# Casts and copies on Pool behind gates, in a planned kernel of attention and two Strassen stages

## The chip, the cores and the metric

The kernel runs on one core of a Trainium2 chip. The metric is the device time of one execution in microseconds (us): the median of the kernel before, over three runs, is 797.23 (795.54 to 802.38).

## What is computed

Sliding-window attention with a linear bias, then two feed-forward blocks over its output. Shapes: q, k, v are (4, 8, 576, 64); w1, w2 (512, 1024), w3 (1024, 1024), w_out (1024, 512); the last two weights (512, 2048) and (2048, 512). All is fp32.

```python
scores = scale * np.matmul(q, k.transpose(0, 1, 3, 2))
bias = slopes[:, None, None] * (-np.abs(rel).astype(np.float32))[None, :, :]
mask = (rel >= 0) & (rel < window)                       # window = 128
scores = np.where(mask, scores + bias[None], -1000000000.0)
scores = scores - np.max(scores, axis=-1, keepdims=True)
attn = np.exp(scores)
attn = attn / (np.sum(attn, axis=-1, keepdims=True) + 1e-09)
x = np.matmul(attn, v)                                   # then reshaped to (2304, 512)
x = (((x @ w1) * (x @ w2)) @ w3) @ w_out
h = np.maximum(x @ w_in, 0.0)
out = h * h @ w_out2
```

## The kernel before

Heads are worked in 16 pairs of one batch (`add_pair`). For a pair, TensorE forms the windowed scores in PSUM (`p_qk`, L473), VectorE adds the bias and takes the row minimum of the negated scores in one custom instruction out of PSUM (`l_min`, L443: "minima" below, ten for a pair), ScalarE takes the exponential with a row sum (`l_exp`, L451), VectorE adds 1e-9 to the sums (the guard, L458) and takes the reciprocal (L459), both in `l_sum`, and VectorE or ScalarE scales the rows (`l_norm`, L267 or L269: "normalizations"). TensorE transposes the result (`p_tr`, L509), ScalarE copies it out of PSUM (`l_pt`), and TensorE multiplies by v (`p_pv`, L533, and `p_pvl`, L549). Some blocks of v are needed on the other half of the partitions, and `l_v` (L417, L418) copies them there. The results leave PSUM in `t_xh`. Pairs before the seventh (`SM`) have guard and reciprocal for each head, later ones once for both.

Beside the attention part the kernel prepares w3 x w_out, since the first block's last two matmuls have no nonlinearity between them. The weights arrive as 64-bit words; `add_words` turns one load of 1 MB (eight of w3, four of w_out, in `load_order`) into fp32 with a Prelu on ScalarE (`conv_g`, L343), a shift on VectorE or ScalarE (`conv_s`, L352) and a merge on VectorE (`conv_m`, L358), and then splits it into two fp32r halves: the cast (`split_h`) and the residue, a subtraction on VectorE (`split_l`, at L211). TensorE multiplies the halves in triples (`p_w34`, L203 to L205): 64 triples in all, of low rank, that fill its idle time. Dummy matmuls fill longer idle times up to 90 us (`p_fill`, L581).

When all pairs are done, the PSUM pools of the attention part are closed (`open_pp`) and products of Strassen's form begin (`add_seven`, L993 to L995, then `p_r` and `p_o`): seven products for each block, of weights and activations that VectorE combines (L778) and ScalarE and VectorE split.

The order on every engine is made at build time by `Plan.run`. Each task has a rank, the engines that it may run on with a cost each, its dependences and the buffers that it takes and gives. The planner takes the ready task of the lowest rank among those that could start soonest; `bias` is added to the cost of an engine in this choice. A cost key "D" means VectorE from SBUF, "d" VectorE from PSUM or small operands, "p" Pool; "D" and "p" exclude each other through `lock`. The engines run their lists in order; semaphores are set by the framework.

```python
bias = dict(d=1.75, D=0.15, a=0.30, p=6)
...
add("sh" + k, rank + 0.1, w_split(1024), lambda e: split_h(key, e), ["cn" + k], ["sp" + k], ["raw" + k])
add("sl" + k, rank + 0.1, w_tt(1024), lambda e: split_l(key, e), ["sh" + k], [], ["raw" + k])
...
add(f"cv{m}", r + RANK["vv"], {"p": 1.1, "D": 0.5}, lambda e: l_v(m, e), [f"ldv{m}"])
```

Of the kernel before, what the change touches and what calls it, by code (L numbers as in the profile page):

```python
# [15 lines left out]
RANK = dict(w34=9, vv=14, w0=-18, c0=-20, cj=6, h0=-42, hs=7, su=6, w12=60, wa=23, wl=5, wb=0, x0=26, mg=5, mgs=1.70, wo=1132, gg=6, yq=1166)  # L16
# [11 lines left out]
SM = 7  # L28
# [4 lines left out]
class Plan:  # L33
# [11 lines left out]
    SLACK = dict(ldw=1, lx=2, ldi=3.0, ldo=3.0, mb=2.00, lg=2.00, lw=4.00, ldv=1.0)  # L45
    STORES = ("sx", "sw", "sg", "sy", "ms", "ss")

    bias = dict(d=1.75, D=0.15, a=0.30, p=6)

    def __init__(self, caps, lat):  # L50
        self.caps, self.lat = caps, lat
        self.tasks = {}
        self.holds = {}

# [6 lines left out]
    def add(self, name, rank, where, fn, deps=(), takes=(), gives=(), keep=0):  # L61

        assert name not in self.tasks, name
        self.tasks[name] = (rank, where, fn, tuple(deps), tuple(takes), tuple(gives), keep)

    def run(self):
# [16 lines left out]
        now = 0  # L83
        while ready:
            cands = []
            for n in ready:
# [13 lines left out]
                for q, w in where.items():  # L100
                    e = q.lower()
# [7 lines left out]
                    for d in deps:  # L109
                        t = max(t, end[d] + self.late(d) * (e != "dma") + (0.0 if on[d] == e and (e != "dma" or d[:2] not in self.STORES) else self.lat[on[d]]))  # L110
# [28 lines left out]
            ready.remove(n)  # L139
            for h in takes:  # L140
                p = pool[self.holds[h][0]]
                p.remove(min(p))
            fin = t + w
            end[n], on[n] = fin, e
            free[e] = fin
            if q in "Dp":
                lock = fin
            for h in gives:
                left[h] -= 1
                last[h] = max(last[h], fin + (self.lat[e] + 0.5 if e == "dma" else 0.0))  # L150
                if left[h] == 0:
                    pool[self.holds[h][0]].append(last[h] + 0.1)
            order.append((n, e, t, fin))
            for u in users.get(n, ()):
                need[u] -= 1
                if need[u] == 0:
                    ready.add(u)
# [5 lines left out]
def fused_kernel(  # L163
# [65 lines left out]
    zero = at.tile([128, 128], F32, name="zero")  # L229
# [54 lines left out]
    def w_split(n):  # L284
        return {"a": 0.12 + n * 0.00088, "p": 0.25 + n * 0.0009}
# [7 lines left out]
    def w_tt(n, engs="Dp"):  # L293
# [3 lines left out]
    def w_ts(n, engs="Dap"):  # L297
# [1285 lines left out]
```

## Time and profile before

| what | value |
|---|---|
| median of three runs | 797.23 us |
| the profiled execution | 796.22 us |
| its span, first to last instruction | 794.4 us |
| granted TensorE clock, of full speed | 0.999 |
| TensorE busy / VectorE / ScalarE / Pool | 783.1 / 632.6 / 513.7 / 3.9 us |

Busy times of TensorE overlap: its matmuls are pipelined and their ends are modelled, so a full share doesn't mean that it had no time to spare. Times in the rows are us from the span's start, unless marked ns. The durations of VectorE and ScalarE reach into the next instruction's, too: what an instruction takes of the engine is read from one start to the next.

### The profile page before, as it was taken

The page shows a single profiled execution, that of the slowest core. Times are in us where ns is not written, and L with a number is a line of the kernel's source. Part 1 is how long each engine was busy: PE and PEld are TensorE (multiplying, and loading weights), DVE is VectorE, ACT ScalarE, POOL GpSimd, SP SyncE. Part 2 cuts the span into 40 slices and gives each one's busy share as a digit, 9 for nine tenths or more (in the row PEclk, how much of TensorE's full clock was granted, in tenths as well). Part 3 has the DMA queues.
Part 4 walks back from the last instruction along what each step waited for, and adds up shares of the span by engine and source line. Part 5 has one row for each costly group of instructions (what it writes and reads, how often), then busy time and mean ns, then how long its engine had stood idle before and what let it go on. Part 6 is the DMA issues. An engine that isn't in the chain of part 4 may idle for free. (4 is left out here: it accounts for less than half of the span.)

```text
span 794.4 us, 17410 instructions
## 1 busy us (share of the span) xinstructions
PE 783.1 (99%) x6664; PEld 741.7 (93%) x6664; DVE 632.6 (80%) x1366; ACT 513.7 (65%) x1102; POOL 3.9 (0%) x19
## 2 busy tenths in 40 slices
PE   8999998999999999999999999999999999999998
PEld 6677776899999999999999999999999999999998
DVE  6999999999887878998889975424678997777762
ACT  7999999775444444655565766546777786666631
POOL 1000000000000000000000000000000000000000
PEclk9999999999999999999999999999999999999999
DMA  9994757635687879666664552535654766454201
GB/s 254 269 310 134 238 161 198 210 122 176 229 269 253 306 241 315 229 222 200 211 207 134 202 189 100 189 120 173 212 193 143 216 176 171 135 140 135 86 27 34
DMA packets 108850, 149.50 MB, mean 188 GB/s; under 512 B 9440, under 2 KB 87776, under 8 KB 106720
## 3 DMA queue, kind: packets, MB, share of 16 engines
q1 hardware_dynamic: 108768, 148.40, 59.1%
q8 instruction: 52, 0.85, 0.4%
q14 instruction: 30, 0.25, 0.1%
HBM read 97.78 MB, written 50.59 MB: 187 GB/s over the span
## 5 line engine op out<-in xcount | busy, mean ns | idle before, releaser
L208 ACT ACTIVATE d<-xa 128x288 f32<-128x288 f32 x128 | 51.6, 409 | 108.9 <-PE xa L995 100.6
L1253 DVE TENSOR_TENSOR D<-xb,D 128x384 f32<-128x384 f32 (+1 forms) x62 | 32.2, 520 | 53.2 <-ACT D L208 26.4
L208 ACT ACTIVATE D<-xa 128x384 f32<-128x384 f32 (+1 forms) x93 | 42.3, 457 | 36.1 <-PE xa L1191 32.4
L451 ACT ACTIVATE e<-e,st 128x192 f32<-128x192 f32 (+1 forms) x144 | 62.3, 439 | 4.9 <-DVE st L443 4.7
L211 DVE TENSOR_TENSOR ww<-fq,ww 128x1024 fp32r<-128x1024 f32 x35 | 42.6, 1223 | 26.3 <-ACT ww L208 26.1
L208 ACT ACTIVATE ww<-fq 128x1024 fp32r<-128x1024 f32 x35 | 37.1, 1059 | 35.7 <-PE xa L1191 19.5
L993 PE MATMUL xa<-xB,u 128*128 128x288 f32 x192 | 57.0, 297 | 0.5 <-DVE d L1042 0.4
L995 PE MATMUL xa<-xB,u 128*128 128x288 f32 x192 | 56.8, 296 | 0.0
L994 PE MATMUL xa<-xB,u 128*128 128x288 f32 x192 | 56.1, 292 | 0.0
L778 DVE TENSOR_TENSOR xA<-xA 128x256 f32<-128x256 f32 (+2 forms) x89 | 52.1, 611 | 0.7
L1326 ACT ACTIVATE D<-D 128x384 f32<-128x384 f32 x72 | 37.3, 521 | 23.0 <-DVE D L1253 22.8
L1014 DVE TENSOR_TENSOR d<-xb,d 128x288 f32<-128x288 f32 x80 | 36.2, 453 | 13.1 <-PE xb L995 8.1
L443 DVE CUSTOM_DVE_ANT_0 e<-s,bw 128x192 f32<-128x192 f32 (+1 forms) x128 | 40.5, 351 | 0.6 <-PE s L473 0.3
L473 PE MATMUL s<-qk 64*64 64x128 f32 (+2 forms) x768 | 36.6, 282 | 2.9 <-DMA qk<-in_qk_dram 2.2
L473 PEld LDWEIGHTS s<-qk 64*64 64x64 f32 x768 | 26.8, 133 | 12.1 <-issue 5.4
L993 PEld LDWEIGHTS xa<-xB,u 128*128 128x128 f32 x192 | 36.1, 188 | 1.0 <-DVE d L1042 0.6
L509 PE MATMUL t<-ident,e 128*128 128x128 f32 x208 | 35.6, 283 | 1.3 <-ACT pt L208 1.1
L509 PEld LDWEIGHTS t<-ident,e 128*128 128x128 f32 x208 | 24.3, 141 | 13.3 <-ACT pt L208 5.9
L994 PEld LDWEIGHTS xa<-xB,u 128*128 128x128 f32 x192 | 36.5, 190 | 0.0
L995 PEld LDWEIGHTS xa<-xB,u 128*128 128x128 f32 x192 | 36.0, 188 | 0.0
L1189 PE MATMUL xa<-yA,v 128*128 128x384 f32 x104 | 35.3, 340 | 0.0
L1191 PE MATMUL xa<-yA,v 128*128 128x384 f32 x104 | 35.2, 339 | 0.0
(267 smaller groups left out, 2920.0 us busy)
## 6 DMA issues: line engine op xcount, KB each, us to landing
s_scr<-D SPq DMA_DIRECT2D x95, 192.0 KB, 1.9
u<-in_w2io_dram SPq DMA_DIRECT2D x32, 512.0 KB, 6.0
xA<-s_scr SPq DMA_DIRECT2D x20, 512.0 KB, 5.4
qk<-in_qk_dram SPq DMA_DIRECT2D x32, 288.0 KB, 5.0
g_scr<-d SPq DMA_DIRECT2D x64, 144.0 KB, 3.1
xA<-g_scr SPq DMA_DIRECT2D x16, 576.0 KB, 5.2
raw<-in_w3t_dram SPq DMA_DIRECT2D x8, 1024.0 KB, 7.2
raw<-in_w_dram SPq DMA_DIRECT2D x8, 1024.0 KB, 7.2
```

The costliest lines, as they stand in the source:

```text
L208: nc.scalar.activation(out=o, in_=i, func=ACTF.Copy)
L211: eng.tensor_tensor(out=o, in0=a, in1=b, op=ALU.subtract)
L443: nc.vector.tensor_tensor_reduce(out=part_of(m, x, rows), in0=ps, in1=bias, op0=ALU.add, op1=ALU.min, scale=-0.125, scalar=3.0e38, accum_o ...
L451: nc.scalar.activation(out=e, in_=e, func=ACTF.Exp, bias=st[:, 0, x:x + 1], scale=-1.0, accum_out=st[:, 1, x:x + 1],)
L473: nc.tensor.matmul(HD[2 * m + r]["s"][g][o, c:c + w], t[h, 0, 64 * q:64 * q + 64], t[h, 1, 64 * k:64 * k + w], start=True, stop=True,)
L509: nc.tensor.transpose(o, e[:, u:u + 2, :].rearrange("p u c -> p (u c)"), ident)
L778: ENG[e].tensor_tensor(out=o(oi), in0=a(ai), in1=b(bi), op=op)
L993: nc.tensor.matmul(o, wh, xh, start=start and c == 0, stop=False, skip_group_check=True)
L994: nc.tensor.matmul(o, wh, xl, start=False, stop=False, skip_group_check=True)
L995: nc.tensor.matmul(o, wl, xh, start=False, stop=c == len(todo) - 1, skip_group_check=True)
L1014: nc.vector.tensor_tensor(out=sb[K, o], in0=sb[K, a], in1=sb[K, o], op=op)
L1326: nc.scalar.activation(out=x, in_=x, func=ACTF.Relu)
```

## The change

The split's cast of w3 and w_out (all loads but the first) and the two copies of v, which become two tasks, may now run on Pool, and there only behind a gate: when the planner places a minimum on VectorE, it looks how long the series of minima from it on will be (`series`), and puts such tasks on Pool as fit into that series by their costs; each gets a dependence on the VectorE instruction ahead of the series (`prevd`), which becomes a semaphore wait of Pool. `after` holds these tasks back until a given pair's minima have been placed. Guard and reciprocal become two tasks (`l_sum`, `l_inv`), and an instruction on VectorE that needs its predecessor's result is charged `OWN` = 0.117 us more, so that the planner puts other work between. `SM` rises from 7 to 13. Ranks, biases and slacks get other values. The new branches for `ND`, `PX` and `VD` are not taken with the values set (-1, 0, 16).

```diff
-RANK = dict(w34=9, vv=14, w0=-18, c0=-20, cj=6, h0=-42, hs=7, su=6, w12=60, wa=23, wl=5, wb=0, x0=26, mg=5, mgs=1.70, wo=1132, gg=6, yq=1166)
+RANK = dict(w34=8, vv=22, w0=-18, c0=-28, cj=6, h0=-42, hs=6, pi=8.00, su=5, w12=60, wa=22, wl=-3, wb=0, x0=26, mg=5, mgs=1.80, wo=1123, gg=0, yq=1172)
...
-SM = 7
+VD = 16
+PA = 1
+PX = 0
+SM = 13
+ND = -1
...
+    OWN = 0.117
+    ROOM = 0.10
...
-    bias = dict(d=1.75, D=0.15, a=0.30, p=6)
+    bias = dict(d=2.00, D=-0.45, a=0.15, p=6)
...
+    def series(self, n):
+        m = int(n.split("_")[1]) // 2
+        return [f"mi{i}_{2 * x + r}" for x in (m, m + 1) for g in ((0, 1, 2), (3, 4)) for r in range(2) for i in g]
...
+                    if q == "p" or "p" in where and self.after.get(n, n) not in (n, *end):
+                        continue
...
+            if e == "d" and n[:2] == "mi":
+                room = t + self.ROOM
+                for k in self.series(n):
+                    i, h = k[2:].split("_")
+                    a = end.get(f"qk{int(i) // 3}_{int(h) // 2}")
+                    if k not in end and a is not None and a + 0.25 <= room + 0.1:
+                        room += tasks[k][1]["d"]
+                while prevd is not None:
+                    best = None
+                    for k in ready:
+                        if "p" not in tasks[k][1]:
+                            continue
+                        s = max(free.get("p", 0.0), free["d"] + 0.25)
...
+                        if s < t + 0.6 + 9e9 * (free.get("p", 0.0) > t) and s + tasks[k][1]["p"] < room:
+                            best = min(best or (9e9,), (tasks[k][0], k, s))
+                    if best is None:
+                        break
+                    _, k, s = best
+                    gate = tasks[k]
+                    tasks[k] = (*gate[:3], (*gate[3], prevd), *gate[4:])
...
-            add("sh" + k, rank + 0.1, w_split(1024), lambda e: split_h(key, e), ["cn" + k], ["sp" + k], ["raw" + k])
+            plan.after["sh" + k] = f"mi4_{2 * 15 + 1}"
+            add("sh" + k, rank + 0.1, w_split(1024) | ({} if early else {"p": 1.05}), lambda e: split_h(key, e), ["cn" + k], ["sp" + k], ["raw" + k])
...
+    def l_inv(m, c):
+        st = stat[m % 2]
         nc.vector.reciprocal(out=st[:, 2, c], in_=st[:, 2, c])
...
-        add(f"cv{m}", r + RANK["vv"], {"p": 1.1, "D": 0.5}, lambda e: l_v(m, e), [f"ldv{m}"])
...
+        if m < VD:
+            for i in range(2):
+                plan.after[f"c{i}v{m}"] = f"mi4_{2 * m + 1}"
+                add(f"c{i}v{m}", r + RANK["vv"], ({"p": 0.31, "D": 0.27}, {"p": 0.41, "D": 0.35})[i], lambda e, i=i: l_v(m, i, e), [f"ldv{m}"])
...
+                add(f"sa{n}", rs, {"d": 0.08}, lambda e, c=c: l_sum(m, c), [f"ex{x}_{m}" for x in ys])
+                add(f"su{n}", rs, {"d": 0.05 + 0.011 * len(ys)}, lambda e, c=c: l_inv(m, c), [f"sa{n}"])
...
+            if n in plan.gated:
+                first = next(i for i in instructions[k:] if i.engine == mybir.EngineType.Pool)
+                before = next(i for i in reversed(instructions[:k]) if i.engine == mybir.EngineType.DVE)
+                tc.add_manual_dep(
+                    first, before.name, mybir.DependencyInfo(mybir.DependencyClass.Sync, mybir.DependencyReason.DATA),
+                    reason="Pool works while VectorE reads PSUM",
+                )
```

The change gives the code other line numbers: the minima are L503, the guard L518, the reciprocal L522, normalizations on VectorE L318, the copies of v L476 and L478, the cast on Pool L331, the residue L262, the transposes L572, the products with v L607 and L623, the triples L254 to L256.

Three places of the new order. On VectorE in the middle of the attention part, a weight load's shift and merge, the copies of v, and guard, reciprocal and normalizations of a pair stand like this before (`raw` is a weight load, `st` the row statistics, `e` the scores):

```order
L352 TENSOR_SCALAR raw_1010<-raw_1010 128x1024
L358 SCALAR_TENSOR_TENSOR raw_1010<-raw_1010 128x1024
L417 COPY v0_162<-v0_162 64x2x128
L418 COPY v0_162<-v0_162 64x2x64
L458 TENSOR_SCALAR st1_165<-st1_165 128x9
L459 RECIPROCAL st1_165<-st1_165 128x9
L267 TENSOR_SCALAR e_1384<-e_1384,st1_165 128x128
L267 TENSOR_SCALAR e_1384<-e_1384,st1_165 128x192 x3
L267 TENSOR_SCALAR e_1384<-e_1384,st1_165 128x128
L267 TENSOR_SCALAR e_1384<-e_1384,st1_165 128x192 x4
```

and this is VectorE around the merge of a weight load after the change (an instruction with only `st` reads out the row minimum of the one ahead of it):

```order
L518 TENSOR_SCALAR st1_165<-st1_165 128x4
L503 ISA e_1113,st1_165<-s_1135,bw_120 64x192
L503 ISA st1_165 64x1
L522 RECIPROCAL st1_165<-st1_165 128x4
L409 SCALAR_TENSOR_TENSOR raw_829<-raw_829 128x1024
L318 TENSOR_SCALAR e_1113<-e_1113,st1_165 128x128
L318 TENSOR_SCALAR e_1113<-e_1113,st1_165 128x192 x3
L518 TENSOR_SCALAR st1_165<-st1_165 128x5
L503 ISA e_1245,st0_164<-s_1192,bz_121 128x128
L503 ISA st0_164 128x1
L522 RECIPROCAL st1_165<-st1_165 128x5
```

The copies of v are gone from here, and a minimum or a merge stands between a guard, its reciprocal and the normalizations that use it. The cast of the merged words stood on ScalarE, here that of the load `raw_1010`:

```order
L208 ACTIVATE pt_1457<-t_1465 128x512
L451 ACTIVATE e_1384,st1_165<-e_1384,st1_165 128x192 x4
L208 ACTIVATE pt_1457<-t_1505 128x512
L208 ACTIVATE w3o_1523<-raw_1010 128x1024
L208 ACTIVATE pl_1537<-t_1526 128x128
```

and Pool, which had only the setup of constants before, now has casts and copies in turn:

```order
L331 CAST w3o_960<-raw_645 128x1024
L478 COPY v1_163<-v1_163 64x2x64
L476 COPY v1_163<-v1_163 64x2x128
L331 CAST w3o_1111<-raw_776 128x1024
L478 COPY v0_162<-v0_162 64x2x64
L476 COPY v0_162<-v0_162 64x2x128
L331 CAST w3o_1242<-raw_829 128x1024
```

Eleven of the twelve casts and 29 of the 32 copies are there. The third place is TensorE at the end of the attention part: the last pair's last transpose and its products with v, before

```order
L509 MATMUL t_2517<-ident_113,e_2309 128x128
L533 MATMUL a_2519<-pt_2471,v1_163 64x192 x2
L533 MATMUL a_2519<-pt_2471,v1_163 64x64 x4
L533 MATMUL a_2529<-pt_2471,v1_163 64x64 x8
L549 MATMUL a_2519<-pt_2471,v1_163 64x64 x2
```

and after

```order
L572 MATMUL t_2508<-ident_113,e_2281 128x128
L607 MATMUL a_2510<-pt_2463,v1_163 64x192 x2
L607 MATMUL a_2510<-pt_2463,v1_163 64x64 x4
L607 MATMUL a_2522<-pt_2463,v1_163 64x64 x8
L254 MATMUL g_2500<-w3o_585,w3o_1989 128x512
L255 MATMUL g_2500<-w3o_585,w3o_1989 128x512
L256 MATMUL g_2500<-w3o_585,w3o_1989 128x512
L623 MATMUL a_2510<-pt_2463,v1_163 64x64 x2
```

A triple of w3 x w_out now stands between the two groups of products with v. From the last pair's first transpose to the first Strassen product there are 13 triples after the change and 10 before, the rest of them behind the transposes and behind the last product with v.

## Rows read from the trace of the kernel before

**Rows 1.** The page's part 1: busy us (share of the span) and count.
```profile
PE 783.1 (99%) x6664; PEld 741.7 (93%) x6664; DVE 632.6 (80%) x1366; ACT 513.7 (65%) x1102; POOL 3.9 (0%) x19
```

**Rows 2.** Stretches: length, busy PE, PEld, DVE, ACT, POOL, clock, DMA share, GB/s.
```profile
100.00:140.00 40.00, 37.77 (x546) 29.79 (x537) 38.94 (x154) 37.29 (x126) 0.00 (x0) 1.00 0.68 186
163.00:200.00 37.00, 36.27 (x270) 35.58 (x270) 36.33 (x68) 22.96 (x45) 0.00 (x0) 1.00 0.49 162
```

**Rows 3.** Waits of the weight loads, 163 us to the end: total, times, longest.
```profile
PEld xb L993 <- DVE d L1014: 2.8, 7, 0.8
```

**Rows 4.** TensorE in order of time, end of the attention part: start, us.
```profile
152.46 0.60 PE L509 MATMUL t<-ident,e 128*128 128x128 f32 x4
...
154.29 0.60 PE L509 MATMUL t<-ident,e 128*128 128x128 f32 x4
...
159.94 0.50 PE L203 MATMUL g<-w3o 128*128 128x512 f32 x1
...
162.83 0.29 PE L993 MATMUL xa<-xA,u 128*128 128x288 f32 x1
```

**Rows 5.** VectorE in order of time, its last normalizations: start, us.
```profile
150.47 1.86 DVE L267 TENSOR_SCALAR e<-e,st 128x128 f32<-128x128 f32 x8
```

**Rows 6.** VectorE in order of time, 100.8 to 104 us: start, us.
```profile
100.89 0.29 DVE L417 COPY v<-v 64x256 f32<-64x256 f32 x1
101.20 0.22 DVE L418 COPY v<-v 64x128 f32<-64x128 f32 x1
101.46 0.29 DVE L443 CUSTOM_DVE_ANT_0 e<-s,bz 128x128 f32<-128x128 f32 x1
...
101.68 0.35 DVE L443 CUSTOM_DVE_ANT_0 e<-s,bw 128x192 f32<-128x192 f32 x1
...
102.23 0.69 DVE L352 TENSOR_SCALAR raw<-raw 128x1024 uint32<-128x1024 uint32 x1
102.85 0.15 DVE L458 TENSOR_SCALAR st<-st 128x9 f32<-128x9 f32 x1
103.04 0.21 DVE L459 RECIPROCAL st<-st 128x9 f32<-128x9 f32 x1
103.28 1.63 DVE L267 TENSOR_SCALAR e<-e,st 128x128 f32<-128x128 f32 x7
```

**Rows 7.** VectorE's groups by shape, 0 to 152.4 us: count | busy us, mean ns | idle before.
```profile
L267 DVE TENSOR_SCALAR e<-e,st 128x192 f32<-128x192 f32 x98 | 25.2, 314 | 0.0
...
L267 DVE TENSOR_SCALAR e<-e,st 128x128 f32<-128x128 f32 x31 | 8.8, 285 | 0.8
...
L459 DVE RECIPROCAL st<-st 128x9 f32<-128x9 f32 x9 | 1.9, 214 | 0.3
...
L458 DVE TENSOR_SCALAR st<-st 128x9 f32<-128x9 f32 x9 | 1.5, 166 | 0.0
L459 DVE RECIPROCAL st<-st 128x5 f32<-128x5 f32 x7 | 1.3, 189 | 0.2
L459 DVE RECIPROCAL st<-st 128x4 f32<-128x4 f32 x7 | 1.2, 178 | 0.2
```

**Rows 8.** DMA queues, 0 to 60 us: packets, MB, share of 16 engines.
```profile
q1 hardware_dynamic: 7155, 16.50, 93.3%
```

**Rows 9.** ScalarE's groups by shape, 0 to 161 us, columns as in rows 7.
```profile
L343 ACT ACTIVATE raw<-raw 128x1024 f32<-128x1024 f32 x15 | 17.1, 1156 | 0.0
...
L208 ACT ACTIVATE w3o<-raw 128x1024 fp32r<-128x1024 f32 x12 | 12.6, 1054 | 0.2 <-DVE raw L358 0.2
...
L269 ACT ACTIVATE e<-e,st 128x192 f32<-128x192 f32 x14 | 6.1, 458 | 0.8 <-DVE st L459 0.8
...
L269 ACT ACTIVATE e<-e,st 128x128 f32<-128x128 f32 x1 | 0.4, 392 | 0.0
```

**Rows 10.** Pool in order of time, 0 to 6 us: start, us.
```profile
1.79 0.28 POOL L242 TENSOR_SCALAR_AFFINE_SELECT bz<-bz 128x128 f32<-128x128 f32 x1
2.04 0.34 POOL L242 TENSOR_SCALAR_AFFINE_SELECT bw<-bw 64x192 f32<-64x192 f32 x1
```

More of the change, by code (lines that the diff above doesn't have):

```diff
@@ L53, in __init__ @@
         self.holds = {}
+        self.after = {}
     def late(self, d):
@@ L83, in run, with commit @@
         now = 0
+        prevd = None
+        self.gated = set()
+        def commit(n, e, t, fin):
+            _, _, _, _, takes, gives, _ = tasks[n]
+            ready.remove(n)
+            for h in takes:
+                p = pool[self.holds[h][0]]
+                p.remove(min(p))
+            end[n], on[n] = fin, e
+            free[e] = fin
+            for h in gives:
+                left[h] -= 1
+                last[h] = max(last[h], fin + (self.lat[e] + 0.5 if e == "dma" else 0.0))
+                if left[h] == 0:
+                    pool[self.holds[h][0]].append(last[h] + 0.1)
+            order.append((n, e, t, fin))
+            for u in users.get(n, ()):
+                need[u] -= 1
+                if need[u] == 0:
+                    ready.add(u)
         while ready:
@@ L374, in fused_kernel, with add_words @@
     w3o = {}
-    def add_words(key, rank, tag, users, keep, lead, after=()):
+    def add_words(key, rank, tag, users, keep, lead, after=(), early=False):
         k = "%s%d" % key
@@ L509, in p_tr, with p_inv @@
             nc.tensor.transpose(o, e[:, u:u + 2, :].rearrange("p u c -> p (u c)"), ident)
+    def p_inv(m):
+        t = PR[m]["t", 4] = ps_t.tile([128, 512], F32, tag="t", name="t")
+        for x in range(4):
+            for r in range(2):
+                nc.tensor.matmul(
+                    t[64 * r:64 * r + 64, 128 * x:128 * x + 128], stat[m % 2][:, 2, 4 * r + x:4 * r + x + 1].to_broadcast([128, 64]), ident,
+                    start=True, stop=True, skip_group_check=True,
+                )
     def l_pt(m, g, e):
@@ L564, in t_xh @@
         for c, q, w in XC[g]:
-            copy(e, to[:, q:q + w], PR[m][g][:, c:c + w])
+            o, i = to[:, q:q + w], PR[m][g][:, c:c + w]
+            if m < ND and q < 512:
+                nc.vector.tensor_tensor(out=o, in0=i, in1=PR[m]["pl"][:, 128 + q:128 + q + w], op=ALU.mult)
+            else:
+                copy(e, o, i)
     def t_xs(m):
@@ L580, in p_fill @@
             n = 512 if us > 0.9 else 128 * int(us / 0.22)
-            nc.tensor.matmul(t[:, 0:n], zero if w else ident, bw[:, 0:2].rearrange("p h c -> p (h c)")[:, 0:n], start=not w, stop=not w)
+            nc.tensor.matmul(t[:, 0:n], zero.to_broadcast([128, 128]) if w else ident, bw[:, 0:2].rearrange("p h c -> p (h c)")[:, 0:n], start=not w, stop=not w)
             us -= n * 0.00168
@@ L644, in add_pair @@
                 [f"tr{g}_{m}"] + ([f"pt0_{m}"] if g else [f"pt0_{m - 1}"] if m else []), [f"pt_{m}"] if g == 0 else [f"pl_{m}"] if g == 3 else [], [f"t{g}_{m}"])
+        if m < ND:
+            hold(f"t4_{m}", "t", 1)
+            add(f"pvi_{m}", r + RANK["pi"], {"pe": w_nat(512) + 0.05}, lambda e: p_inv(m), [f"su{n}" for n in (heads if m < SM else heads[:1])] + lt, [f"t4_{m}"])
+            add(f"pt4_{m}", r + 8.5, w_copy(512, True), lambda e: l_pt(m, 4, e), [f"pvi_{m}", f"pt3_{m}"], [], [f"t4_{m}"])
         for g, w in enumerate((320, 256)):
@@ L916, in hi @@
                 t = wc[fi, part] = new("u", [128, 2, w], F32R)
-                copy(e, t[:, 0], full()[:, o:o + w])
+                scopy(e, t[:, 0], full()[:, o:o + w])
             def lo(e, part=part, w=w, o=o):
```

100 lines of the change are left out of this document (57 added, 43 removed).

## The prediction

> **What bounds the kernel now.** I read the page's busy shares first, then stretches of the span, then the ends of the stages in the timelines, and last the groups of the engine that is left. By the page TensorE is 99% busy [rows 1], and a reader could stop there. The stretches say otherwise: from 100 to 140 us VectorE is busy 38.94 of 40 us and ScalarE 37.29, while TensorE's 37.77 are full of modelled overlaps [rows 2]. That is the attention part, where TensorE has slack (fillers keep it running). After it TensorE waits for almost nothing: the longest sum of its weight loads' waits from 163 us to the end is 2.8 us [rows 3], and the matmuls there are the same in number in both kernels. So the time is the moment of the first matmul of the Strassen products, plus a fixed remainder of 794.4 - 162.8 = 631.6 us. That first matmul starts at 162.83 [rows 4]; the last attention pair's first transpose starts at 152.46, just behind VectorE's last normalization, which ends at 150.47 + 1.86 = 152.33 [rows 4, 5]. The attention part ends when VectorE has got through its list, and a tail of 10.4 us follows on TensorE.
>
> **The change on VectorE.** A duration in the trace is longer than the step from one start to the next: a minimum of 192 columns lasts 0.35 us and the shift at 102.23 lasts 0.69, but the add behind it starts 0.62 later [rows 6]. An instruction that doesn't need its predecessor's result starts about 0.08 before that one ends; one that does starts about 0.04 after the end: the add lasts 0.15 and steps 0.19, the reciprocal lasts 0.21 and steps 0.24 [rows 6]. I count all that stands on VectorE before its last normalization in the order of either kernel and price it by steps.
> - Copies of v: 30 before, 3 after (1 large, 2 small). Steps are 0.31 and 0.26 [rows 6]: 14 x 0.31 + 13 x 0.26 = 7.7 us off.
> - Guard and reciprocal: 23 pairs before, at duration + 0.035 each. With adds of 0.165 and reciprocals of 0.214, 0.189 and 0.178 [rows 7] that is 9 x 0.45 + 7 x 0.42 + 7 x 0.41 = 9.9 us. After, there are 29 pairs (3, 13 and 13 of 9, 5 and 4 columns, as pairs of heads 7 to 12 are now summed head by head), and 28 have another instruction between the two. At duration - 0.08 that is 3 x 0.22 + 13 x 0.19 + 13 x 0.18 = 5.5, and 0.2 for the pair left adjacent: 5.7. So 4.2 off, though there are six pairs more.
> - Normalizations: eight more of 192 columns (0.314 - 0.08 = 0.23) and five fewer of 128 (0.285 - 0.08 = 0.21) [rows 7]: 0.8 on.
> - Two shifts of weight words go to ScalarE: 2 x 0.62 = 1.2 off [rows 6]. One product operand comes before the end and one combination falls behind it; I cost the two at +0.3.
>
> Sum: -7.7 - 4.2 + 0.8 - 1.2 + 0.3 = -12.0 us, if VectorE waits no more than it does. The cumulative list tells where: before the seventh pair it is only some 1 us shorter, so the gain comes after the stretch from 0 to 60 us in which the DMA queue is 93.3% busy [rows 8]. The faster pace therefore doesn't run into that queue, and I cost the loads at nothing; if the early pace were set by them, that 1 us would be lost.
>
> **On ScalarE.** Eleven of twelve casts leave: 11 x (1.054 - 0.10) = 10.5 off. Eight normalizations of 192 leave (8 x 0.36 = 2.9), five of 128 come (1.5), two weight words' Prelu (2 x 1.05 = 2.1) and one cast of a combined weight (of the same size as the casts, 0.95) come: in all 8.9 off [rows 9]. ScalarE had 2.7 us of slack in 40 where VectorE had 1.1 [rows 2], so VectorE stays the later one, but not by much.
>
> **On Pool.** No cast runs on Pool in this trace. Its select over 128 columns lasts 0.28 and over 192 0.34 [rows 10]: 0.94 ns a column. Without a fixed part 1024 columns take 0.96 us; with it 0.28 + 0.84 = 1.12; in proportion to the longer row 0.34 / 192 x 1024 = 1.81. I take 1.1, nearest to the line through both rows. Copies of 128 and 256 columns are then 0.28 and 0.40, and Pool's whole load is 11 x 1.1 + 29 x 0.35 = 22 us. The residue (the subtraction of the cast) waits for Pool on VectorE, in order, and everything behind it waits too. Between the merge of the words and the residue the new order has 1.6 to 7.7 us of VectorE's steps; the tightest cast has six minima of 192 columns, 6 x (0.35 - 0.08) = 1.6 us [rows 6]. A cast of 1.1 with 0.3 for the two semaphores fits, one of 1.81 would make VectorE wait up to 0.5 each time, 11 x 0.5 = 5.5 us. Copies of v are asked for by the last attention products of their pair, a transposition and three evacuations later, and cost nothing. A second cost can't be bounded from a row, because Pool and VectorE never work side by side here: whether they slow each other. Below it is nothing; above it is all of Pool's 22 us, when VectorE stands still for each of its instructions. The gate lets Pool start behind the instruction ahead of a series of minima, whose one operand is in PSUM, and the series is mostly as long as the instruction. I take 1.0 us in all for both, mostly for adds and normalizations that meet the end of a cast.
>
> The Trainium skill speaks against this change in two places. "GPSIMD Engine Reference", section "Performance versus the Vector engine", gives 1.03 cycles an element for the shortest loop bodies and about 1.8 at best for longer ones; at 1.8 a cast would be 1.54 us (an estimate from that page), and VectorE would wait 0.2 us for the tightest cast, at most 11 x 0.2 = 2.2 us for all; the slope of our two rows is nearer to the first. "SBUF — State Buffer", section "Who interferes with whom", says that VectorE and GpSimd hold one pair of ports exclusively, against any VectorE instruction with two inputs in SBUF or in a two-port mode, and that the loser stands still for the whole of it; by it minima out of PSUM are safe and the rest isn't. No run so far shows it; what it would cost is the second rival.
>
> **The tail on TensorE.** In the order, between the last pair's first transpose and the first product stand 13 triples of w3 x w_out after the change, 10 before. A transpose with two triples steps 154.29 - 152.46 = 1.83, and the last four triples take 162.83 - 159.94 = 2.89, 0.72 each [rows 4]. Three more cost 2.2 us. They are real work that TensorE would do earlier if it could, but the shorter attention part leaves it less room.
>
> **Sum.** -12.0 (VectorE) + 2.2 (tail) + 1.0 (Pool) = -8.8 us: first product at 154.0, span 785.6. Behind it I cost the change at nothing: the same matmuls, TensorE's waits there are 2.8 us at most to win, and VectorE has four combinations of w1, w2 more behind it when the products begin (12 against 8), so that the tight stretch from 163 to 200 (36.33 of 37 busy [rows 2]) starts no worse. The profiled execution took 796.2, with 1.8 outside its span, so 787.4 by its own time; it lies 1.0 under the median of 797.2. Against the median I say 788.4.
>
> **Rivals.**
> - ScalarE takes over as the bound. For: its list shrinks by 8.9, VectorE's by 12.0, and it loses only 2.7 us in 40. Against: that slack, some 10 us over the attention part, can shrink too. Then -8.9 + 2.2 = -6.7 us: 790.5.
> - The shared path decides: VectorE stands still while Pool works. Place: the norms, shifts, merges and adds that meet a cast or a copy of v. Price: up to 22 us, against 12.0 saved on VectorE and 2.2 given back in the tail. At a share of (12.0 - 2.2) / 22 = 45% there is no gain; beyond it the kernel is slower, at the full price by 12 us: 809. For: none of Pool's starts is tied to VectorE's later instructions, so nothing stops a late cast from meeting them. Against: each start is tied to the instruction before a series, and most series are longer than 1.1 us.
> - Half of that, with casts nearer to 1.8 us: 5.5 us of waits at the residues takes the place of the copies removed: -12.0 + 2.2 + 5.5 = -4.3, so 793.
> - The change doesn't do what it says: the products start 9 us earlier, but their operands (VectorE busy 36.33 of 37 there) are late, and TensorE waits for them. For: VectorE is all but full until 200. Against: the list above. Price: at most what was won, likely 3 to 5 us: 792.
>
> **How the numbers follow.** Forecast (784 to 790) 0.50; ScalarE 0.17; late casts 0.13; late operands 0.12; slower 0.08. One per cent, 8 us, is about what a measurement of this kernel can tell from no change; the line to "faster" is at 789.3. Of the forecast's half some 0.42 lies under it, a third of the ScalarE case and a little of the others too, and a gain over 12 us isn't excluded when VectorE's own gaps shrink: 0.52. Slower by over 1% needs a share of Pool's time above 80%: 0.05. The rest, 0.43, is within 1%. Range: 783 (the sum without tail and Pool terms, and 2 us of gaps gone) to 795 (late casts and late operands together reach it).
>
> **What would show it.** Right: casts on Pool of 1.0 to 1.2 us; v copies gone from VectorE; steps of adds and reciprocals of about 0.08 and 0.10 to 0.13; VectorE's last normalization near 141 to 142; first product near 154; as long from there to the end as before. Wrong: minima, norms or adds on VectorE longer than before while Pool is busy (shared path); VectorE idle at a residue with Pool as releaser (late casts); VectorE idle for ScalarE's exponentials (ScalarE bound); TensorE waits of more than 5 us between 154 and 200 (late operands).

## The result, and the profile after

| | before | after |
|---|---|---|
| median (lowest to highest) | 795.13 us (794.18 to 802.38), 6 runs | 785.34 us (783.12 to 789.94), 6 runs |
| ratio, 95% interval | | 0.9867 [0.9823, 0.9911] |
| the profiled execution, its span | 796.22, 794.4 us | 783.12, 781.3 us |
| VectorE's last normalization ends | 152.33 | 139.00 |
| first matmul of the products | 162.83 | 151.60 |
| from there to the end of the span | 631.6 | 629.7 |

The kernel is 1.3% faster: 9.8 us by the medians, where 8.8 was forecast. (The ratio takes in all runs of both kernels, so it isn't the quotient of the medians, 0.9877.) The two profiled executions stand 13.1 us apart, since the one of after is the fastest of its six runs. All but 1.9 us of these 13.1 lie ahead of the first product.

The page's part 1 after the change (busy us, share of the span, count), for [rows 1]:

```profile
PE 773.2 (99%) x6646; PEld 738.2 (94%) x6646; DVE 622.2 (80%) x1353; ACT 504.9 (65%) x1087; POOL 25.2 (3%) x59
```

Pool has 40 instructions more, 21.4 us of work. TensorE's and VectorE's busy time fall by some 10 us each; on TensorE that says little, because its busy time counts modelled overlaps.

Stretches after the change, the last one from just behind the first product (columns as in [rows 2]):

```profile
60.00:100.00 40.00, 39.60 (x611) 31.38 (x612) 39.53 (x171) 39.32 (x138) 9.57 (x16) 1.00 0.83 248
...
153.00:190.00 37.00, 36.97 (x278) 36.57 (x277) 33.14 (x61) 22.11 (x45) 0.00 (x0) 1.00 0.47 155
```

In the middle of the attention part VectorE (39.53 of 40) and ScalarE (39.32) are now both all but full: either could be the bound there. In the 37 us behind the first product VectorE has room (33.14), where before it had 36.33 of 37 [rows 2].

VectorE in order of time, its last normalizations (for [rows 5]):

```profile
137.34 1.66 DVE L318 TENSOR_SCALAR e<-e,st 128x128 f32<-128x128 f32 x7
```

TensorE in order of time, from the last pair's first transpose to the first product (for [rows 4]):

```profile
138.86 0.65 PE L572 MATMUL t<-ident,e 128*128 128x128 f32 x4
...
151.60 0.29 PE L1086 MATMUL xa<-xA,u 128*128 128x288 f32 x1
```

The tail from the last normalization to the first product is 151.60 - 139.00 = 12.6 us, where it was 10.5: the 13 triples instead of 10.

Pool's groups, 6 to 142 us (columns as in [rows 7], and the releasers of the idle time):

```profile
L331 POOL CAST w3o<-raw 128x1024 fp32r<-128x1024 f32 x11 | 11.4, 1037 | 52.0 <-issue 13.5 <-DVE raw L409 10.0 <-PE t L572 8.2
L476 POOL COPY v<-v 64x256 f32<-64x256 f32 x15 | 5.9, 396 | 15.8 <-PE a L623 7.1 <-DVE e L318 3.6 <-DVE st L518 1.8
L478 POOL COPY v<-v 64x128 f32<-64x128 f32 x14 | 4.1, 291 | 35.1 <-PE t L572 10.7 <-DVE st L518 7.4 <-DVE st L522 6.3
```

A cast takes 1.04 us, close to the 1.1 taken. The copies take 0.40 and 0.29 us. No residue on VectorE waits for Pool.

VectorE's groups, 0 to 139.2 us (for [rows 7]):

```profile
L503 DVE CUSTOM_DVE_ANT_0 e<-s,bw 128x192 f32<-128x192 f32 x96 | 30.9, 346 | 0.3 <-PE s L536 0.3
L318 DVE TENSOR_SCALAR e<-e,st 128x192 f32<-128x192 f32 x106 | 26.9, 313 | 0.0
...
L518 DVE TENSOR_SCALAR st<-st 128x5 f32<-128x5 f32 x13 | 3.0, 228 | 0.0
```

VectorE's waits up to its last normalization (total, times, longest), before and after; the first row of both views, 4.9 and 5.0 us for Pool's constants, is left out:

```profile
DVE e L443 <- PE s L473: 2.1, 3, 1.2
DVE e L443 <- PE t L509: 1.6, 1, 1.6
```

```profile
DVE e L503 <- PE s L536: 1.6, 3, 1.1
DVE e L503 <- PE t L572: 0.7, 1, 0.7
DVE raw L403 <- DMA raw<-in_w_out_dram: 0.4, 1, 0.4
```

The means in the groups above are those of before but for one group: the 13 guards of 5 columns have a mean of 228 ns, and a mean can hide one outlier. VectorE in order of time shows it, and beside it Pool in order of time:

```profile
60.08 0.29 DVE L503 CUSTOM_DVE_ANT_0 e<-s,bz 128x128 f32<-128x128 f32 x1
...
60.30 1.04 DVE L518 TENSOR_SCALAR st<-st 128x5 f32<-128x5 f32 x1
61.25 0.34 DVE L503 CUSTOM_DVE_ANT_0 e<-s,bw 128x192 f32<-128x192 f32 x1
```

```profile
60.27 1.04 POOL L331 CAST w3o<-raw 128x1024 fp32r<-128x1024 f32 x1 [3.05 <-DMA qk<-in_qk_dram]
```

A cast began 0.03 us before a guard of five columns, and the guard stood still until the cast had ended: 1.04 us instead of 0.16. The planner had let it stand there: a guard has the cost key "d", and only "D" is kept apart from Pool. Besides it one normalization of 128 columns took 631 ns instead of 281. These two are all that lengthens beside Pool: 0.88 + 0.35 = 1.2 us. Of the minima, 94 overlap with Pool's work and last 347 and 289 ns, as the others do. The Trainium skill ("SBUF — State Buffer", section "Who interferes with whom") states just this: a VectorE operation in a two-port mode (it names `tensor_scalar`, which guard and normalization are, among those that can enter one) and one of GpSimd exclude each other for a whole instruction, and one outside these modes that reads at most one operand from SBUF is free; the 1036 ns and the minima's 347 agree.

### The profile page after: what moved, and what is told of

Its sections match the earlier page's. It is cut to its first block, busy times and chain, and to the rows that moved or that the text cites. A ratio compares the mean times of both kernels' runs of the same rounds, so it can differ in the third digit from the quotient of the medians.

```text
span 781.3 us, 17418 instructions
## 1 busy us (share of the span) xinstructions
PE 773.2 (99%) x6646; PEld 738.2 (94%) x6646; DVE 622.2 (80%) x1353; ACT 504.9 (65%) x1087; POOL 25.2 (3%) x59
## 5 line engine op out<-in xcount | busy, mean ns | idle before, releaser
L511 ACT ACTIVATE e<-e,st 128x128 f32<-128x128 f32 (+1 forms) x144 | 62.4, 442 | 5.4 <-DVE st L503 5.3
L262 DVE TENSOR_TENSOR ww<-fq,ww 128x1024 fp32r<-128x1024 f32 x35 | 42.7, 1223 | 26.3 <-ACT ww L259 26.1
L503 DVE CUSTOM_DVE_ANT_0 e<-s,bw 128x192 f32<-128x192 f32 (+1 forms) x128 | 40.3, 347 | 0.6 <-PE s L536 0.3
L572 PE MATMUL t<-ident,e 128*128 128x128 f32 x208 | 35.1, 282 | 1.7 <-ACT pt L259 1.5
L572 PEld LDWEIGHTS t<-ident,e 128*128 128x128 f32 x208 | 23.9, 140 | 13.7 <-ACT pt L259 7.1
L1282 PE MATMUL xa<-yA,v 128*128 128x384 f32 x104 | 35.3, 340 | 0.0
L1284 PE MATMUL xa<-yA,v 128*128 128x384 f32 x104 | 35.2, 339 | 0.0
L1283 PE MATMUL xa<-yA,v 128*128 128x384 f32 x104 | 35.2, 339 | 0.0
L536 PE MATMUL s<-qk 64*64 64x128 f32 (+2 forms) x768 | 34.4, 281 | 0.1
```

The source lines that it names most:

```text
L262: eng.tensor_tensor(out=o, in0=a, in1=b, op=ALU.subtract)
L503: nc.vector.tensor_tensor_reduce(out=part_of(m, x, rows), in0=ps, in1=bias, op0=ALU.add, op1=ALU.min, scale=-0.125, scalar=3.0e38, accum_o ...
L511: nc.scalar.activation(out=e, in_=e, func=ACTF.Exp, bias=st[:, 0, x:x + 1], scale=-1.0, accum_out=st[:, 1, x:x + 1],)
L572: nc.tensor.transpose(o, e[:, u:u + 2, :].rearrange("p u c -> p (u c)"), ident)
L1282: nc.tensor.matmul(o, wh, xh, start=start, stop=False, skip_group_check=True)
L1283: nc.tensor.matmul(o, wh, xl, start=False, stop=False, skip_group_check=True)
```

## The experiments

The same kernel before ran beside each group of kernels on its chip (medians 796.7, 796.5 and 795.9 us), and ratios are to it. The change itself has two ratios, 0.9867 above and 0.9881 in its second measurement below; differences from the change are given against both, in per cent of 796 us. The edits are to the changed kernel, unless said.

**What the two moves to Pool are worth.** In the first three kernels the order of all tasks is the changed kernel's; only the engine of some is another, and what stays on Pool keeps its gate. A plan made for these engines could lose less; that was not tried.

```diff
             plan.tasks[n][2](e)
# copies_vector: ahead of that line
+            if n[0] == "c" and n[2] == "v":
+                e = "d"
# casts_scalar: ahead of that line
+            if n[:2] == "sh" and e == "p":
+                e = "a"
# both_back: both edits
```

> The changed kernel with the same order, but the 29 copies of v are issued on VectorE at the places where the planner put them for Pool. Theory (VectorE's list sets the time): 14 copies of 256 columns x 0.31 and 15 of 128 x 0.26 come back, 8.2 us, so about 793 to 794 where the changed kernel has 785.3, and VectorE's last normalization near 147 instead of 139.0. Rival (the order alone made the gain, and VectorE has room): under 2 us more than the changed kernel. Rival (ScalarE is the bound): VectorE's additional work falls into its waits, 2 to 4 us more.

Measured: 793.26 us (10 runs, 790.48 to 796.33), ratio 0.9955 [0.9933, 0.9978]: 6 to 7 us slower than the change. VectorE's last normalization ended at 150.3, not near 147, since its waits were 2.4 us longer than in the first profile of the change; the first product came at 162.8. In this order the copies are the greater part of the gain, as reckoned.

> The changed kernel with the same order, but the eleven casts are issued on ScalarE at the places where the planner put them for Pool. 11 x 0.95 = 10.5 us come back to ScalarE. Theory (VectorE is the bound, ScalarE second by a few us of slack): ScalarE's slack of some 10 us takes a part, so 4 to 8 us more than the changed kernel, 789 to 793, with VectorE idle for ScalarE's exponentials. Rival (ScalarE is as much a bound as VectorE): the full 10 us, 795 or more. Rival (casts on ScalarE were hidden anyway): under 2 us more.

Measured: 791.07 us (4 runs, 789.91 to 791.84), ratio 0.9931 [0.9907, 0.9955]: 4 to 5 us slower. The longest of VectorE's waits from 0 to 147 us, behind that for Pool's constants (total, times, longest):

```profile
DVE st L518 <- ACT e L511: 4.9, 6, 1.0
```

This row is the forecast's first rival in the flesh: with the casts on it ScalarE comes last, and VectorE's guards wait 4.9 us for its exponentials. In the change that row is not there. So the cast's move doesn't shorten VectorE's list at all and still pays.

> The changed kernel with the same order, with the 29 copies on VectorE and the eleven casts on ScalarE at the places where they stood for Pool. What is left of the change is the new order, with guard and reciprocal apart. The copies alone cost 7.1 us and the casts alone 5.1 by ratio. Theory (two engines bound in turn): together 10 to 13 us, 796 to 799, about the kernel before or a little slower, although guard and reciprocal are apart; then all of the gain needs Pool. Rival (one engine's longer list hides the other's): 8 us or less, 794 or less, and a part of the gain is the order's.

Measured: 792.49 us (10 runs, 791.94 to 800.94), ratio 0.9987 [0.9959, 1.0015]. That is 8 to 10 us slower than the change by the ratios but 6 to 7 by the medians, since two of its ten runs took over 800. The sum of the two single moves is 10 to 12, so whether they add is open. By its ratio, 0.9987 with an interval that holds 1, the new order without Pool's part can't be told from the kernel before. VectorE waited 2.4 us for exponentials, half as long as with the casts alone, as one would expect where VectorE's own list is longer; that was not tried by itself.

**What the gate is worth.**

```diff
-            if n in plan.gated:
+            if False:
```

> The changed kernel with the same order on all engines, without the added dependence of Pool's casts and copies on the VectorE instruction ahead of a series of minima. Theory (Pool and VectorE exclude each other outside the minima): casts start as soon as the words are merged and meet normalizations, shifts and residues; in the changed kernel one guard lasted 1.04 us and one normalization 0.63 beside Pool, 1.2 us in all, and without the gate I expect three to eight such meetings, 2 to 5 us more, 787 to 790, with normalizations of up to 1 us. Rival (such meetings are rare, as merges are mostly followed by minima): within 1 us, 784.5 to 786.5.

Measured: 788.88 us (4 runs, 787.96 to 792.89), ratio 0.9914 [0.9881, 0.9948]: about 3 us slower, though its interval overlaps with the change's, so that the time alone doesn't settle it. The durations do. VectorE's and Pool's groups, to 144 us:

```profile
L318 DVE TENSOR_SCALAR e<-e,st 128x192 f32<-128x192 f32 x106 | 31.2, 351 | 0.0
L503 DVE CUSTOM_DVE_ANT_0 e<-s,bw 128x192 f32<-128x192 f32 x96 | 30.8, 346 | 0.3 <-PE s L536 0.3
```

```profile
L331 POOL CAST w3o<-raw 128x1024 fp32r<-128x1024 f32 x11 | 13.1, 1186 | 69.3 <-DVE raw L409 22.8 <-issue 20.6 <-ACT sg L259 6.7
```

The normalizations of 192 columns grow from a mean of 313 to 351 ns; the 20 that meet Pool's work last 528 on the mean, up to 1099. All that lengthens comes to 6.5 us on VectorE, in 16 instructions where three to eight were expected, against 1.2 in two with the gate, and Pool's casts are held too, up to 1984 ns. The minima stay at 346.

**How hard the shared path bites.** Two kernels add work to Pool in the kernel before, without gates, and leave out nothing:

```diff
+    junk = at.tile([128, 256], F32, name="junk")
+    for _ in range(300):
+        nc.gpsimd.tensor_copy(out=junk, in_=bw[:, 0])
# pool_sets: 380 times, with
+        nc.gpsimd.memset(junk, 0.0)
```

> The kernel before with 300 added copies of 256 columns on Pool from the bias table into a tile that nobody reads, one after the other and waiting for nothing: Pool busy over most of the attention part. Measures what Pool costs VectorE without any gate. Theory (one pair of ports, held for a whole instruction by either): normalizations, copies, shifts, residues and combinations of VectorE last up to 0.4 us longer, minima and reciprocals as before, and Pool's copies stretch too; the kernel 15 to 40 us slower. Rival (they share without loss): all of VectorE's durations within 3%, time within 1%.

> The kernel before with 380 added sets of 256 columns on Pool, which write and don't read, one after the other, waiting for nothing. Beside the copies on Pool, normalizations rose from 0.314 to 0.476 us, adds from 0.166 to 0.308, residues from 1.220 to 1.264, and minima and reciprocals stayed. Theory (reading and writing ports are separate, and an instruction with two inputs in SBUF takes only the reading one): normalizations, adds and copies, which run in a doubled mode, are longer again, residues and combinations are not. Rival (any instruction of Pool holds all of it): residues longer too.

Measured, one run each: 825.66 us with the copies, 808.9 with the memsets. VectorE's groups up to its last normalization in the kernel before, then with the copies, then with the memsets (to 172 us, where it ended at 165.5):

```profile
L267 DVE TENSOR_SCALAR e<-e,st 128x192 f32<-128x192 f32 x98 | 25.2, 314 | 0.0
...
L211 DVE TENSOR_TENSOR w3o<-raw,w3o 128x1024 fp32r<-128x1024 f32 x12 | 14.6, 1220 | 0.1
...
L211 DVE TENSOR_TENSOR xA<-u,xA 128x576 fp32r<-128x576 f32 x7 | 5.1, 754 | 0.1
```

```profile
L271 DVE TENSOR_SCALAR e<-e,st 128x192 f32<-128x192 f32 x98 | 41.6, 477 | 0.0
L447 DVE CUSTOM_DVE_ANT_0 e<-s,bw 128x192 f32<-128x192 f32 x96 | 31.0, 348 | 0.3 <-PE s L477 0.3
L211 DVE TENSOR_TENSOR w3o<-raw,w3o 128x1024 fp32r<-128x1024 f32 x12 | 15.2, 1264 | 0.1
...
L211 DVE TENSOR_TENSOR xA<-u,xA 128x576 fp32r<-128x576 f32 x7 | 5.9, 869 | 0.1
...
L463 DVE RECIPROCAL st<-st 128x9 f32<-128x9 f32 x9 | 1.9, 214 | 0.3
```

```profile
L271 DVE TENSOR_SCALAR e<-e,st 128x192 f32<-128x192 f32 x98 | 35.5, 415 | 0.0
L447 DVE CUSTOM_DVE_ANT_0 e<-s,bw 128x192 f32<-128x192 f32 x96 | 31.0, 348 | 0.3 <-PE s L477 0.3
L211 DVE TENSOR_TENSOR w3o<-raw,w3o 128x1024 fp32r<-128x1024 f32 x12 | 14.6, 1214 | 0.1
...
L211 DVE TENSOR_TENSOR xA<-u,xA 128x576 fp32r<-128x576 f32 x8 | 5.9, 753 | 0.1
```

With Pool copying all the time a normalization takes 477 instead of 314 ns and subtractions of two SBUF operands grow by 44 and 115 ns; with Pool only writing, the subtractions stay as they were and the normalizations still grow to 415. Minima out of PSUM and reciprocals (214) stay as they were beside either. The last normalization came 178.0 - 152.3 = 25.7 us later beside the copies, 13.1 beside the memsets. Against Pool's 155 us of copying, its own holds included, that is a share of 17%: beside a Pool that works without aim VectorE loses a sixth of Pool's time, and in the kernel without gates 6.5 of 25 us, a quarter. The forecast's second rival needed 45%.

**What guard and reciprocal apart are worth.**

```diff
# adjacent: l_sum issues both, l_inv nothing
+        nc.vector.reciprocal(out=st[:, 2, c], in_=st[:, 2, c])
# no_guard: l_sum issues nothing
-        nc.vector.tensor_scalar(out=st[:, 2, c], in0=st[:, 1, c], scalar1=1.0e-9, scalar2=None, op0=ALU.add)
...
+        nc.vector.reciprocal(out=st[:, 2, c], in_=st[:, 1, c])
```

> The changed kernel with the same order, but each reciprocal stands right behind its guard. Theory: 28 pairs lose the instruction between them, each reciprocal then starts 0.04 after the guard's end instead of 0.08 before it; what follows the reciprocal mostly doesn't need it. 28 x 0.12 = 3.3 us more on VectorE, so about 788 to 789. Rival (the earlier reciprocal lets normalizations and transposes start earlier, or VectorE's waits take it up): within 1 us of the changed kernel.

Measured: 786.28 us (4 runs, 785.82 to 787.09), ratio 0.9875 [0.9848, 0.9902]: within 1 us of the change on either side. In its profile the last normalization ended at 141.5. That is 2.5 us later than in the first profile of the change, and 0.3 earlier than in the second. VectorE's waits up to there, behind that for Pool's constants:

```profile
DVE e L503 <- PE s L536: 1.6, 3, 1.1
DVE st L518 <- ACT e L511: 0.2, 1, 0.2
```

The second profile is the change once more:

> The changed kernel once more, beside the runs of this call: 785 to 787, 0.985 to 0.989 of the kernel before.

Measured: 786.63 us (6 runs, 784.07 to 788.96), ratio 0.9881 [0.9856, 0.9905]. VectorE's waits up to its last normalization in this second profile, for those of the first above:

```profile
DVE raw L403 <- DMA raw<-in_w_out_dram: 2.6, 1, 2.6
DVE e L503 <- PE s L536: 2.3, 3, 1.8
DVE e L503 <- PE t L572: 0.7, 1, 0.7
```

The same program's last normalization ends 2.9 us later, at 141.86: the first pair's minima began 0.7 later, and a shift waited 2.2 longer for one load of w_out, which landed 11.3 us after its issue instead of 9.0. The end of VectorE's list in a single profile can't tell 2 us of work from a late load; the end less the waits can, as shown below.

> The changed kernel with the same order, without the guard: the reciprocal reads the row sum itself. The largest score of a row contributes exp(0) = 1 to its sum, and 1 + 1e-9 is 1 in fp32, so the values stay. Theory (VectorE's list still sets the time): 29 guards at a step of about 0.12 are 3.5 us, with the one that stood beside a cast for 1.04 us some 4; 3 to 4 us less than the changed kernel, 782, last normalization near 135.5. Rival (the guard stands where VectorE waits for ScalarE's exponentials, and the wait stays): within 1 us of the changed kernel.

This kernel leaves the guard out, the addition of 1e-9 to a sum that is at least 1. Measured: 785.03 us (5 runs, 784.29 to 786.07), ratio 0.9861 [0.9839, 0.9883]: 0.5 to 1.6 us faster than the change, which its interval doesn't separate from none; 3 to 4 were expected. Its last normalization ended at 139.5, where 135.5 was expected. Its waits say where the rest went (to 142 us, behind that for Pool's constants):

```profile
DVE e L503 <- PE s L536: 2.4, 4, 1.1
DVE raw L403 <- DMA raw<-in_w_out_dram: 1.4, 1, 1.4
DVE raw L403 <- DMA raw<-in_w_dram: 1.0, 1, 1.0
DVE raw L403 <- DMA raw<-in_w3t_dram: 1.0, 1, 1.0
DVE e L503 <- PE t L572: 1.0, 1, 1.0
```

The shift of weight words stands at a fixed place in VectorE's list; when the list gets there sooner, it waits for the load: 3.4 us here (the 1.0 for `in_w_dram` just behind the last normalization), 0.4 and 2.6 in the two profiles of the change.

**VectorE's list and its waits apart.** Here the list is the end of the last normalization less VectorE's waits ahead of it (idle times of over 0.15 us, the 5 us for Pool's constants among them), in us, from one profile of each kernel:

| kernel | last normalization | waits | list |
|---|---|---|---|
| before | 152.33 | 8.58 | 143.75 |
| the change, first profile | 139.00 | 7.63 | 131.37 |
| the change, second profile | 141.86 | 10.51 | 131.35 |
| copies on VectorE | 150.34 | 10.06 | 140.28 |
| casts on ScalarE | 146.40 | 15.13 | 131.27 |
| copies and casts back | 148.44 | 8.81 | 139.63 |
| no gate | 143.77 | 7.20 | 136.57 |
| guard and reciprocal adjacent | 141.53 | 6.79 | 134.74 |
| no guard | 139.53 | 11.00 | 128.53 |

The change's two profiles have the same list; 2.9 us of waits part them. So the list shows what the ends and the times don't. With guard and reciprocal adjacent it is 3.4 us longer, where 3.3 was expected; without the guard it is 2.8 shorter, and the waits are longer by more than that; without the gate it is 5.2 longer. With copies and casts back it is still 4.1 shorter than in the kernel before, by the order alone; but 13 triples follow it instead of 10, and the tail from the last normalization to the first product is 12.4 us instead of 10.5.

**Trying to keep what the loads take.** Three kernels were planned anew: without the guard as a task (guardless), the same with the conversion of the weights ranked later (guardless_later, `c0` in `RANK` from -28 to -24), and the change itself, guard and all, with `c0` at -20 (later_words). The edit of guardless in the planner, beside that of no_guard:

```diff
-                add(f"sa{n}", rs, {"d": 0.08}, lambda e, c=c: l_sum(m, c), [f"ex{x}_{m}" for x in ys])
...
+                add(f"su{n}", rs, {"d": 0.05 + 0.011 * len(ys)}, lambda e, c=c: l_inv(m, c), [f"ex{x}_{m}" for x in ys])
```

> The guard is left out as in the run without it on the old order (sums are at least 1, so the values stay), but the planner now knows it and makes the order anew. There the time won on VectorE went into three waits of the shift for weight loads (3.4 us). Theory (the order can put other work in front of those shifts): waits for loads under 1.5 us, last normalization near 136, 782 to 783.5. Rival (the loads themselves set the early pace, at 93 to 95% of the queue): as without replanning, 784 to 786, with the waits elsewhere.

> As the run before, and the weight words' conversion ranks four later (-24 instead of -28), while the loads keep theirs. Theory (loads arrive late for the conversion): waits of the shift for loads under 0.5 us, 781.5 to 783. Rival (conversions put off come back as triples of w3 x w_out behind the attention part): no better than 784, with more triples between the last pair's first transpose and the first product than the 13 of the changed kernel.

> The changed kernel with the guard, planned anew with the conversion's rank back at -20, as in the kernel before (-28 in the change). Tells what the earlier conversion in the change is worth. Theory (earlier conversions only shorten the tail of triples by 1 to 2 us and cost waits for loads): within 2 us of the changed kernel, 784 to 788. Rival (the earlier conversion is a main part of the gain): 790 or more.

| | time, runs | ratio | last normalization | triples from the last pair's first transpose on | first product | TensorE's stalls behind it |
|---|---|---|---|---|---|---|
| the change, first profile | 785.34, 6 | 0.9867 [0.9823, 0.9911] | 139.0 | 13 | 151.6 | 3.6 |
| guardless | 790.33, 6 | 0.9915 [0.9888, 0.9942] | 139.7 | 17 | 155.6 | 5.5 |
| guardless_later | 799.22, 12 | 1.0044 [1.0021, 1.0067] | 137.1 | 19 | 155.8 | 14.6 |
| later_words | 792.99, 10 | 0.9948 [0.9929, 0.9967] | 139.8 | 18 | 155.8 | 7.6 |

(The stalls are the sums of what the steps from matmul to matmul exceed the usual step of their shape by.) All three missed what their theories expected; the rivals of guardless_later and later_words, more triples behind the attention part and 790 us or more, came out. VectorE finished no later than between the two profiles of the change (139.0 and 141.9), in guardless_later earlier, and still the kernels were slower than the change by 3 to 14 us (ratios). A later conversion leaves more triples for the tail, at 0.7 us each (18 instead of the change's 13 in later_words, 19 instead of guardless's 17 in guardless_later); that guardless has 17 comes of the new plan. With the old rank of the conversion 5 to 6 us of the change's gain are gone in later_words, although Pool has its part: the new rank, or the order that comes of it, belongs to the cause, too. And in guardless_later TensorE then stands idle for operands. Its stretch from 160 to 180 us (columns as in [rows 2]), its waits from 140 to 200 us on TensorE, and VectorE in order of time ahead of the longest:

```profile
160.00:180.00 20.00, 15.15 (x94) 13.87 (x93) 19.19 (x33) 12.21 (x21) 0.00 (x0) 0.91 0.31 111
```

```profile
PE xa L1085 <- ACT d L259: 3.7, 4, 1.7
PE xa L1087 <- DVE u L262: 3.3, 1, 3.3
```

```profile
165.63 0.69 DVE L403 TENSOR_SCALAR raw<-raw 128x1024 uint32<-128x1024 uint32 x1
166.23 1.22 DVE L262 TENSOR_TENSOR u<-raw,u 128x1024 fp32r<-128x1024 f32 x1
```

The products have begun, and VectorE still shifts and splits weight words; the product's weights wait for that residue. Which of the planner's choices makes it so isn't settled: a rank shifts the whole order, and no kernel changed the conversion alone. No kernel tried is clearly faster than the change.

## Why the prediction was right, point by point

- **The time is the first product plus a fixed remainder.** Right: 11.2 of the 13.1 us between the profiles lie ahead of the first product. The remainder was costed at no change and shrank by 1.9 us in the first profile; TensorE's stalls there fell from 5.5 to 3.6. In the second profile of the change the remainder is 784.6 - 154.5 = 630.1.
- **VectorE's list, -12.0 us.** Nearly right as a sum, not in all its parts. The list above is 12.4 us shorter with 1.2 lost beside Pool in it, so 13.6 without. By steps from start to start, waits left out: copies -7.7, as reckoned; guard and reciprocal -2.6 instead of -4.2; shifts -2.2 instead of -1.2; normalizations 0.4 on instead of 0.8; and merges (-0.6) and minima (-1.1) step shorter, too, which the forecast hadn't.
- **Copies of v, -7.7.** Confirmed by the steps, and by the kernel with the copies on VectorE: 6 to 7 us slower, its list 8.9 us longer.
- **Guard and reciprocal apart, -4.2.** Right in kind, mis-sized: 9.9 us before, as reckoned, but 7.2 after (without the 0.9 for which one guard was held) instead of 5.7. The reciprocals' steps are nearly as reckoned (0.10 for one of five columns in the place of 0.22). The guards step 0.12 on the mean instead of 0.08, because behind eight of them the next instruction, though it isn't their reciprocal, starts only 0.03 after their end; why these eight is open. That the separation shortens the list is shown by the kernel with the two adjacent, whose list is 3.4 us longer. In the time it isn't: that kernel was within 1 us of the change, and one profile of it doesn't say where the 3.4 us went.
- **Pool, +1.0, and the cast at 1.1.** Right: 1.2 us and 1.04 us. The lengthened ones are a guard and a normalization that meet a cast, as said, though the guard met its start and not its end. That by the rule of the ports only minima are safe was too wide: reciprocals lasted as long beside a copying Pool as before (214 ns). The section of the Trainium skill that spoke for 1.54 us ("GPSIMD Engine Reference", "Performance versus the Vector engine") has 1.03 cycles an element as its other figure; by it a cast is 0.88 us (an estimate from that page), and the measured 1.04 lies nearer to that.
- **Loads at nothing.** This step failed. "The faster pace doesn't run into that queue" was read from where the gain arises; but the shift stands 2.6 us idle for a load at 36 us in one profile and 0.4 in another. VectorE waited for no load in the attention part of the profile before. The 2.2 us between the two profiles are most of their difference ahead of the first product; whether loads also make the spread of the other runs is not shown.
- **The tail, +2.2.** Right: 12.6 us instead of 10.5, with 13 triples.
- **The sum, and luck.** List with its holds, waits, tail and remainder are -12.4 - 0.9 + 2.1 - 1.9 = -13.1 us in the first profile and -12.4 + 1.9 + 2.1 - 1.5 = -9.9 in the second, where -11.0 + 0 + 2.2 + 0 = -8.8 was forecast. That the medians came within 1 us of it is in part luck: guard and reciprocal gave less than reckoned, shifts, merges, minima and the remainder gave more, and the waits moved either way.
- **What the forecast left out.** The changed ranks got no price. The kernel later_words shows that one of them has one: with the conversion's old rank in the plan VectorE's last normalization still comes at 139.8, within the change's range, but the kernel is 5 to 6 us slower by what stands behind it.
- **The rivals.** ScalarE as the bound came within reach and didn't win: it is busy 39.32 of 40 us, VectorE waits for none of its exponentials, and the kernel with the casts on it shows what the rival would have been. The shared path is real and dear per event (0.9 us for a guard of 0.16), but the gate leaves two events; without it the loss is 6.5 us on VectorE and about 3 in the time. Late casts and late operands didn't come: the residue never waits for Pool, and VectorE has 33.14 of 37 us behind the first product. Late operands do cost guardless_later most of what it loses (stalls of 14.6 us) and later_words a part (7.6), so that rival exists, only in other orders than this one.

## What to carry to other kernels

Two engines that share a path can work side by side if the starts of the one are tied to series on the other that don't use it; the test is that the durations beside the second engine stay the same, and outliers are to be looked for one by one, since a mean of 13 hides a stall of six times the length. Before crediting a shorter list, look for what in it waits for a load at a fixed place and what is left to do behind it: here three kernels whose list ended in the change's range or ahead of it lost 3 to 14 us behind it. And take the waits off before comparing the ends of two lists: in two profiles of one program the ends differed by 2.9 us, and the lists without their waits by 0.02.

## What the runs showed of the hardware

A small VectorE instruction isn't safe beside Pool for being small: a guard on 128 x 5 elements waited out a whole cast, 1036 ns instead of 161. The hold goes both ways: without gates Pool's casts grew up to 1984 ns, and in the kernel with 300 copies single ones up to 1627 where the median was 401. Pool's writes alone hold the normalizations (314 to 415 ns) but not subtractions of two SBUF operands (1220 and 1214). Reciprocals, which like the guard have one operand in SBUF, were held by neither.

In the kernel guardless_later TensorE was idle for 3.3 us, and the granted clock fell behind that idle time. Its stretches (columns as in [rows 2]):

```profile
164.00:166.00 2.00, 0.17 (x2) 0.00 (x0) 1.97 (x5) 2.00 (x5) 0.00 (x0) 1.00 0.24 86
166.00:168.00 2.00, 0.49 (x2) 0.50 (x3) 2.00 (x3) 0.60 (x2) 0.00 (x0) 0.87 0.83 217
168.00:170.00 2.00, 2.00 (x10) 2.00 (x10) 1.92 (x3) 1.09 (x2) 0.00 (x0) 0.50 0.89 365
...
172.00:174.00 2.00, 2.00 (x17) 2.00 (x16) 1.75 (x4) 1.75 (x4) 0.00 (x0) 1.00 0.00 0
```

From 168 to 170 us it is 0.50, the lower level of 1.2 GHz, and 10 matmuls run where 17 do from 172 to 174 at full clock. This wait for operands so cost more than its own length.
